# A global-filter layer and a two-layer network on one core: the inverse step of the next token group moves into a packed step of the third unit

## The chip, the cores and the metric

The kernel runs on one core of a Trainium2 chip. The metric is the device time in microseconds (us) of the program on that core. Engines are named as in the profile: PE is the matrix engine (PEld is its weight load), DVE the vector engine, ACT the scalar engine, POOL the GpSimd engine; SP issues most of the DMAs.

## The reference, cut to what matters

```python
X = np.fft.rfft(x, axis=1)                 # x: (8, 3008, 256)
Y = X * (filt_r + 1j * filt_i)[None]
t = np.fft.irfft(Y, n=3008, axis=1).reshape(24064, 256)
h = t @ w_in                               # (24064, 2048)
g = h - np.tanh(h)
out = g @ w_out                            # (24064, 256)
```

Everything is computed in float32.

## The kernel before

**The transform.** The length 3008 is split as 64 by 47, and the transform of a batch element is done in four stages with tables held in the kernel. The *forward* step (`first`, or in packed form `split_first`) transforms along the 64 and stores to the DRAM tensor `ct1`. The *middle* step (`middle`) takes a quarter of the frequencies at a time, o = 0 to 3: `packed` transforms along the 47 ("there"), the filter is multiplied in, and `packed` transforms back ("back") to the DRAM tensor `ct2`. The *inverse* step (`last`) transforms along the 64 back again and leaves the tokens of one group, transposed, in the tile `ut`; `combine` then makes four sums of its blocks, in `tu`.

**Packed steps.** `last`, `packed` and `split_first` use matmuls that fill only a part of the PE array: 64 by 64 (line 582, tile `pu`), 24 by 32 (line 401, tile `pm`) and 32 by 32 (line 340, tile `pm`), several of them side by side. All other matmuls of the main loop fill the array, 128 by 128. The program calls each Python matmul of float32 data as two instructions, so that a packed step of 32 matmuls shows as x64.

**Groups and units.** The main loop goes through 48 token groups, six chunks c for each of eight batch elements p. A group has 512 tokens (448 for c = 0) and its blocks are w = 256 (224) wide. A group is done in four units u = 0 to 3, each with a quarter of the hidden features, and U counts units. In unit U the loop interleaves, by hand, four streams:

- `up(U)`: the first matrix product, with seven block products in place of eight (a scheme of Strassen's kind). They run in the order 1, 2, 6, 5, 7, 4, 3 over the PSUM banks x, y, x, z, x, x, z. Bank x is added to step by step: after product 1 ACT copies it (`s1`), after 6 it copies it again (`u2`), after 7 once more (`u3`), and after 4 DVE does. All three ACT copies are line 629. The next product into bank x cannot begin until the copy before it has ended.
- `shrink(U-1)`: h - tanh(h) in the form h times a square: ACT runs an arctangent (line 735), a tanh (738) and a square (741) for each half of h, DVE multiplies (745), and POOL makes the four sums `t` (lines 603 to 606).
- `down(U-2)`: the second matrix product, again with seven products, into the banks o0 to o3 (line 795). Its four pieces, products (1, 2), (3, 5), (6, 7) and (4), are let in by the calls `d()`. In the last unit of a group the sums of these banks are taken off; line 834 is the last reader of bank o3.
- `t(k)`, k = 0 to 4: five places in a unit where a step of the transform for a later group or batch element is let in, and where four stores are issued on SP's queue.

What a place `t(k)` holds is fixed: the inverse step of the next group at (u, k) = (3, 2); "there" at (2, 0) and "back" at (1, 3), by the list `kinds`; the pieces of `split_first` at the places (c, u, k) of `SPLIT_AT`. In a unit the order at its start is: product 1, product 2, copy `s1`, `t(0)`, first `d()`, first activations (`shrinks`), and then product 6.

**Banks.** There are eight PSUM banks: x, y, z, t and o0 to o3. A packed step borrows four of them, the inverse step two.

**Weight sums.** The seven products need sums of weight blocks. `sums(u)` makes the four for one quarter of a weight matrix, on DVE (lines 228 and 231). Those of quarters 0, 1, 2 and 4 are made among the conversions of the weights, before unit 6; those of 3, 5, 6 and 7 in units 6 and 7.

Of the kernel before, what the change touches and what calls it, by code (L numbers as in the profile page):

```python
# [116 lines left out]
def kernel(  # L117
# [104 lines left out]

        return jobs

    def sums(u):

        w = (wu if u < 4 else wd)[:, :, 256 * (u % 4):256 * (u % 4) + 256]
        V.tensor_add(w[:, 4], w[:, 6], w[:, 3])
        yield
        for to, one_in, less in ((5, 4, 0), (2, 1, 5), (6, 0, 6)):  # L230
            V.tensor_sub(w[:, to], w[:, one_in], w[:, less])  # L231
            yield

    def begun(tiles, job, queue=nc.sync):
        j = converted(tiles, *job, queue)
# [5 lines left out]
    def weights(tiles, jobs, queue, began, ahead, after=()):  # L241

        began += [begun(tiles, job, queue) for job in jobs[len(began):ahead]]
        yield
        for k in range(len(jobs)):
            pending[0] = len(jobs) - k
            for n, _ in enumerate(began[k]):
                yield
                if (after or k > 1) and n == 2 and k + 1 < len(jobs):
                    next(began[k + 1])  # L250
            if k + ahead < len(jobs):
                began.append(begun(tiles, jobs[k + ahead], queue))
            pending[0] = len(jobs) - k - 1
            for u in dict(after).get(k, ()):
                yield from sums(u)

    def load_x(t, b, r, n):

# [47 lines left out]
    def split_first(b, z):  # L306

        quarters = [slice(32 * k, 32 * k + 32) for k in range(4)]
        for c, tags in enumerate((("t", "o1", "y", "o0"), ("t", "o3", "o1", "o2"),
                                  ("t", "o1", "y", "o0"))):  # L310
            f = tr.tile([128, XH, 128], F32, tag="f", bufs=2, name="f")[:, 0:2]
            f = f.rearrange("p a (b n) -> p (a b) n", n=32)
            nc.sync.dma_start(f, split_d[:, 256 * c:256 * c + 256])
            x0, x1 = (tr.tile([128, XH, DM], F32, tag="x", bufs=2, name="x_sb") for _ in range(2))
            for h, t in enumerate((x0, x1)):
                at = b * SEQ + 32 * h * NR
                for g in range(2):
                    r = 2 * FH * c + FH * g
                    low, high = quarters[g], quarters[2 + g]
                    nc.sync.dma_start(t[low], dram(x.tensor, (at + r) * DM,  # L320
                                                   [[NR * DM, 32], [1, FH * DM]]))
                    lo = int(r == 0)
                    if lo:
                        nc.sync.dma_start(t[high, 0], dram(x.tensor, at * DM,
                                                           [[NR * DM, 32], [1, DM]]))
                    nc.sync.dma_start(t[high, lo:FH], dram(x.tensor, (at + NR - r - lo) * DM,
                                                           [[NR * DM, 32], [-DM, FH - lo], [1, DM]]))
            yield
            both = tr.tile([128, 2, 2, DM], F32, tag="a1", bufs=1, name="a1")
            even = both.rearrange("p v n c -> p (v n) c")  # L330
            V.tensor_add(even, x0, x1)
            yield
            V.tensor_sub(x1, x0, x1)
            yield
            banks = z(tags)
            for n in range(2):
                for k, (bank, part) in enumerate(zip(banks, quarters)):
                    for j, to in enumerate(quarters):
                        m, odd = 2 * (j // 2) + n, j % 2
                        nc.tensor.matmul(bank[to, n], f[part, 2 * m + odd],  # L340
                                         (x1 if odd else even)[part, m], start=True, stop=True)
            made = both, x0.rearrange("p (v n) c -> p v n c", v=2)
            other = x1[:, 0:2]
            for g, a1 in enumerate(made):
                ACT.copy(a1[:, 1], banks[2 + g])
            ACT.copy(other, banks[1])
            for g, a1 in enumerate(made):
                V.tensor_add(a1[:, 0], other if g else banks[0], a1[:, 1])
                V.tensor_sub(a1[:, 1], other if g else banks[0], a1[:, 1])
                outs[:0] = [(dram(ct1[b], ((1 - j % 2) * NH + 2 * FH * c + FH * g +  # L350
                                           2 * (j // 2)) * DM,
                                  [[2 * NH * DM, 32], [64 * NH * DM, 2], [1, 2 * DM]]),
                             a1[part].rearrange("p v n c -> p v (n c)"))
                            for j, part in enumerate(quarters)]
                yield

    SPLIT_AT = {(0, 0, 2), (0, 1, 0), (0, 1, 3), (1, 1, 1), (1, 1, 4), (2, 0, 2),
                (3, 0, 2), (4, 2, 0), (4, 2, 2), (4, 3, 0), (5, 0, 2), (5, 1, 0), (5, 1, 3),
                (5, 2, 2)}

    def parts(t, b, g, first_block=0, n=4, step=1):
# [25 lines left out]
    def packed(banks, o, weight, data):  # L387

        ahead, whole, late = [], [], []
        for q, bank in enumerate(banks):  # L390
            part = slice(PAD * q, PAD * q + NH)
            for col in range(4):
                to, at = bank[PAD * col:PAD * col + PAD], data(q, col)[part]
                plain, special = (wide[part, weight(q, col, last)] for last in (0, 1))
                if o == 3 and 3 == (col if weight is WAYS[0] else q):
                    ahead.append((to[:, 0], plain, at[:, 0:DM]))
                    late.append((to[:, 1], special, at[:, DM:2 * DM]))
                else:
                    whole.append((to.rearrange("p n c -> p (n c)"), plain, at))
        for to, weights_of, at in ahead + whole + late:  # L400
            nc.tensor.matmul(to, weights_of, at, start=True, stop=True)  # L401
# [205 lines left out]

    hs, gs = {}, {}

    def up(U, d, e, s, t):  # L610

        i, u = divmod(U, 4)
        b, tu, w = uts[i]
        rhs = [b[0][0], b[1][0], b[1][1], tu[:, 3, 0:w], tu[:, 0, 0:w], tu[:, 1, 0:w],
               tu[:, 2, 0:w]]
# [24 lines left out]
        mm(X, 1, True)  # L640
        mm(Y, 2, True)
        s1 = copied("s1")
        t(0)
        d()
        shrinks(0)
        V.tensor_add(h[:, 0, :, 0:w], Y, s1)
        e()
# [358 lines left out]
    with tc.tile_pool(name="tr", bufs=2) as tr, tc.manual_schedule():  # L1006
# [16 lines left out]
        with tc.tile_pool(name="pro", bufs=1) as pro, \  # L1023
# [201 lines left out]
            for g in range(last_g + 1):  # L1225
# [30 lines left out]
                if g == 3:  # L1256
# [5 lines left out]
            next(fs)  # L1262
            convert(100)
            late = weights(tiles1, jobs[5:], G, ahead, 3,
                           after={6: (0,), 8: (1,), 10: (2, 4)})
            next(late)
            for _ in first1(x1):
                pass
# [2 lines left out]
        with tc.tile_pool(name="dn", bufs=2) as dn, \  # L1271
# [4 lines left out]

            def zd2(name, shape):
                return [ps.tile(shape, F32, tag=tag, bufs=1, name=name) for tag in "ty"]

            def zd4(tags):  # L1280
                return [ps.tile([128, 2, DM], F32, tag=tag, bufs=1, name="pm") for tag in tags]
# [59 lines left out]
            for U in range(total + 2):  # L1341
                i, u = divmod(U, 4)
                if U == 6:
                    assert not pending
                    late = (None for u in (3, 5, 6, 7) for _ in sums(u))
                if U == 3:
                    G.dma_start(mats[:, 0:10 * PAD], wide_d[0:KM])
                if U < total:
                    p, c = groups[i]
                    if c == 0 and u == 0 and 0 < p < BATCH - 1:  # L1350
                        plan += STAGES
                    if u == 0 and i + 1 < len(groups) and c + 1 < NC:
                        e2s[i + 1] = load_e2(*groups[i + 1])
                    if u == 2 and i + 1 < len(groups) and c + 1 == NC:
                        assert not plan
                        e2s[i + 1] = load_e2(*groups[i + 1])
                    if u == 3 and c + 1 == NC and p + 3 < BATCH:
                        firsts[p + 3] = split_first(p + 3, zd4)
                        next(firsts[p + 3])
                    if u == 3 and c + 1 == NC and p + 2 < BATCH:  # L1360
                        mids[p + 2] = middle(p + 2, zd4)
                        next(mids[p + 2])
# [11 lines left out]
                def d():  # L1374

                    next(dw, None)
# [10 lines left out]
                def t(k):  # L1387
# [7 lines left out]
                    if i == 1 and pos == LEAD - 7:  # L1395
# [1 line left out]
                        mids[1] = middle(1, zd4)  # L1397
                        next(mids[1])
                        plan.extend(STAGES)
                    if (u, k) == (3, 2) and i + 1 < len(groups):  # L1400
                        next(last(i + 1, z2))
                    elif due and due[0] <= pos and (U < 4 or u < 3 and k == 2):
                        due.pop(0)
                        next(firsts[2])
                    elif (c, u, k) in SPLIT_AT and 0 < p < BATCH - 2:
                        next(firsts[p + 2])
                    elif plan and plan[0] == kinds.get((u, k)):
                        plan.pop(0)
                        next(mids[p + 1])
# [58 lines left out]
```

## Time and profile before

| What | us |
|---|---|
| median of three runs | 2559.25 |
| lowest and highest run | 2557.61, 2559.39 |
| the profiled execution, its own time | 2556.2 |
| span of the profiled execution | 2554.4 |
| DVE busy | 1875.8 (73%) |
| ACT busy | 1667.1 (65%) |
| POOL busy | 1484.3 (58%) |

The busy time of PE and the other rows that the argument needs stand in the prediction. In the timelines each row has the start, the length, the engine, the line, the operation, what it writes and reads, and its shape with the number of merged instructions. A matmul's length is modelled and overlaps with the next one, so the distance between starts is what counts: four full matmul instructions of 256 columns start 0.86 us before the next four.

### The profile page before, as it was taken

The numbers are of one execution on the slowest core, as the hardware profiler recorded it, in microseconds if no ns is written. First come the engines' busy times: TensorE is split into PE (matmuls) and PEld (weight loads), VectorE is DVE, ScalarE is ACT, GpSimd is POOL, SyncE is SP. The second block draws the span as 40 slices with busy tenths as digits, with TensorE's granted clock in tenths as the row PEclk, the third lists the DMA queues.
The fourth block names the chain that finished last, engine by engine and source line by source line (L and its number), as shares of the span: only waits on it lengthen the run. The fifth ranks groups of instructions, "written<-read, shape, count | busy, mean of one in ns | idle before, by whom it ended". The sixth has DMA issues, their size and how long they took to land.

```text
span 2554.4 us, 44623 instructions
## 1 busy us (share of the span) xinstructions
PE 2535.7 (99%) x17072; PEld 2173.1 (85%) x17072; DVE 1875.8 (73%) x2262; ACT 1667.1 (65%) x2498; POOL 1484.3 (58%) x1129
## 2 busy tenths in 40 slices
PE   9999999999999999999999999999999999999998
PEld 8678889888898888988888888888889888898887
DVE  6887776887678876888668886688866777555555
ACT  4666666666666666666666666666666666666665
POOL 5356665666466665666555665566645666555552
PEclk9999999999999999999999999999999999999999
DMA  8963224322343323342233322443123322110110
GB/s 233 287 163 103 65 53 109 102 65 61 83 102 91 81 64 94 80 111 59 72 95 99 85 63 61 108 100 97 36 67 85 94 66 52 26 32 18 25 22 19
DMA packets 333828, 212.43 MB, mean 83 GB/s; under 512 B 231841, under 2 KB 304959, under 8 KB 329957
## 3 DMA queue, kind: packets, MB, share of 16 engines
q1 hardware_dynamic: 318471, 184.18, 29.3%
q0 software_dynamic: 11616, 17.44, 2.5%
q10 hardware_dynamic: 3518, 7.87, 0.9%
q8 instruction: 136, 2.23, 0.4%
q14 instruction: 87, 0.71, 0.1%
HBM read 128.75 MB, written 83.39 MB: 83 GB/s over the span
## 4 chain that ended last, share of the span: by engine, by line
PE 94%; DMA 3%; DVE 1%; ACT 1%; issue 0%; SPq 0%; POOL 0%; ACTq 0%; POOLq 0%; DVEq 0%
PE o L795 44%; PE x L623 25%; PE z L623 12%; PE y L623 6%; PE pm L401 3%; PE pu L582 2%; DMA x<-in_x_dram 1%; PE pm L340 1%; DMA filt<-in_filt_r_dram 1%; DMA ct<-a 0%; PE o L857 0%; PE pf L297 0%; DMA filt<-filt 0%; DMA ct<-e 0%; DVE wd L231 0%
## 5 line engine op out<-in xcount | busy, mean ns | idle before, releaser
L795 PE MATMUL o<-t,wd 128*128 128x256 f32 (+1 forms) x3008 | 763.4, 376 | 0.0
L603 POOL TENSOR_TENSOR t<-h 128x512 f32<-128x512 f32 (+1 forms) x186 | 305.4, 1642 | 712.7 <-DVE h L745 704.3
L745 DVE TENSOR_TENSOR h<-h,y 128x1024 f32<-128x1024 f32 (+1 forms) x384 | 580.2, 1511 | 160.1 <-ACT y L741 156.6
L795 PEld LDWEIGHTS o<-t,wd 128*128 128x128 f32 x3008 | 568.8, 190 | 85.8 <-POOL o L827 15.1
L623 PE MATMUL x<-tu,wu 128*128 128x256 f32 (+1 forms) x2256 | 576.1, 378 | 0.0
L795 PE MATMUL o<-h,wd 128*128 128x256 f32 (+1 forms) x2256 | 573.4, 377 | 0.2 <-DVE h L745 0.2
L795 PEld LDWEIGHTS o<-h,wd 128*128 128x128 f32 x2256 | 425.6, 190 | 71.3 <-issue 18.4
L629 ACT COPY s<-x 128x512 f32<-128x512 f32 (+1 forms) x188 | 108.6, 578 | 565.0 <-PE x L623 564.5
L623 PEld LDWEIGHTS x<-tu,wu 128*128 128x128 f32 x2256 | 423.3, 190 | 56.9 <-issue 3.9
L738 ACT ACTIVATE y<-y 128x1024 f32<-128x1024 f32 (+1 forms) x384 | 399.4, 1040 | 12.1
L741 ACT ACTIVATE y<-y 128x1024 f32<-128x1024 f32 (+1 forms) x384 | 399.9, 1041 | 4.6
L735 ACT ACTIVATE y<-h 128x1024 f32<-128x1024 f32 (+1 forms) x384 | 400.4, 1043 | 2.5 <-DVE h L671 1.7
L604 POOL TENSOR_TENSOR t<-h,t 128x512 f32<-128x512 f32 (+1 forms) x186 | 313.9, 1688 | 14.6
L606 POOL TENSOR_TENSOR t<-h,t 128x512 f32<-128x512 f32 (+1 forms) x186 | 303.8, 1633 | 0.0
L605 POOL TENSOR_TENSOR t<-h 128x512 f32<-128x512 f32 (+1 forms) x186 | 289.8, 1558 | 0.0
L629 ACT COPY u<-x 128x512 f32<-128x512 f32 (+1 forms) x376 | 213.3, 567 | 57.0 <-PE x L623 54.1
L671 DVE COPY h<-x 128x512 f32<-128x512 f32 (+1 forms) x188 | 127.8, 680 | 127.2 <-PE x L623 127.1
L623 PE MATMUL y<-ut,wu 128*128 128x256 f32 (+1 forms) x752 | 190.2, 375 | 0.7 <-ACT a L299 0.7
L623 PE MATMUL z<-tu,wu 128*128 128x256 f32 (+1 forms) x752 | 190.2, 375 | 0.4 <-DVE h L679 0.4
L623 PE MATMUL z<-ut,wu 128*128 128x256 f32 (+1 forms) x752 | 190.2, 375 | 0.4 <-DVE h L663 0.4
L623 PE MATMUL x<-ut,wu 128*128 128x256 f32 (+1 forms) x752 | 190.1, 375 | 0.0
L663 DVE TENSOR_TENSOR h<-z,u 128x512 f32<-128x512 f32 (+1 forms) x188 | 127.3, 677 | 72.0 <-ACT u L629 71.1
(208 smaller groups left out, 2809.1 us busy)
## 6 DMA issues: line engine op xcount, KB each, us to landing
ft<-filt SPq DMA_DIRECT2D x28, 1024.0 KB
ct<-nn SPq DMA_DIRECT2D x56, 512.0 KB
e<-ct SPq DMA_DIRECT2D x47, 512.0 KB
a<-ct SPq DMA_DIRECT2D x112, 192.0 KB
out_dram<-ot SPq DMA_DIRECT2D x1248, 16.0 KB
x_sb<-in_x_dram SPq DMA_DIRECT2D x110, 128.0 KB
ct<-a SPq DMA_DIRECT2D x60, 128.0 KB
ct<-x_sb SPq DMA_DIRECT2D x60, 128.0 KB
```

Source lines behind the costliest of these rows:

```text
L603: by.tensor_sub(t[0], b[0][1], b[0][0])
L604: by.tensor_sub(t[1], b[1][1], t[0])
L605: by.tensor_sub(t[2], b[1][1], b[0][1])
L606: by.tensor_sub(t[3], b[1][0], t[1])
L623: nc.tensor.matmul(bank[:, k], wu[:, q - 1, (2 * u + k) * 128:(2 * u + k + 1) * 128], rhs[q - 1], start=(first and k == 0), stop=True, ski ...
L629: ACT.copy(t, X)
L671: V.tensor_copy(h[:, 2, :, 0:w], X)
L735: ACT.activation(y[k], ht[k], AF.Arctan, scale=TURN)
L738: ACT.activation(y[k], y[k], AF.Tanh, scale=BEND)
L741: ACT.activation(y[k], y[k], AF.Square, scale=SCALE, accum_out=y_sums[:, 2 * U + k // 2:2 * U + k // 2 + 1])
L745: V.tensor_mul(ht[k], ht[k], y[k])
L795: nc.tensor.matmul(product(q), wd[:, q - 1, (2 * u + k) * 128: (2 * u + k + 1) * 128], rhs[q - 1][:, k], start=(u == 0 and k == 0 and q == ...
```

## The change

`merged(U)` is true for the third unit (u = 2) of the groups 2 to 46, but not of the group (0, 5). In such a unit `t(0)` and the first `d()` run ahead of products 1 and 2, and the inverse step of the next group is let in there, at (2, 0), in the banks y and x; the step that was at (2, 0) before follows it at once. In the other groups the inverse step stays at (3, 2), in the banks t and y. The packed order of "there" goes over the banks t, o1, o2, o3 and no longer over t, o3, o1, o2. The last piece of `split_first` with matmuls moves from (5, 1, 3) to (5, 2, 0), with other banks, and the first takes its banks in another order. The inverse step's operands `e2` are loaded at u = 0 of the group before, but for (0, 5). Of the weight sums, three of four for the quarters 3, 5, 6 and 7 are made among the conversions, and only the last of each, which overwrites a block that is in use until then, in unit 6.

```diff
-    def sums(u):
+    def sums(u, n=4):
...
-        for to, one_in, less in ((5, 4, 0), (2, 1, 5), (6, 0, 6)):
+        for to, one_in, less in ((5, 4, 0), (2, 1, 5), (6, 0, 6))[:n - 1]:
...
+    def last_sum(u):
+
+        w = (wu if u < 4 else wd)[:, :, 256 * (u % 4):256 * (u % 4) + 256]
+        V.tensor_sub(w[:, 6], w[:, 0], w[:, 6])
...
-        for c, tags in enumerate((("t", "o1", "y", "o0"), ("t", "o3", "o1", "o2"),
-                                  ("t", "o1", "y", "o0"))):
+        for c, tags in enumerate((("t", "y", "o1", "o0"), ("t", "o3", "o1", "o2"),
+                                  ("t", "o3", "o1", "o2"))):
...
-                (3, 0, 2), (4, 2, 0), (4, 2, 2), (4, 3, 0), (5, 0, 2), (5, 1, 0), (5, 1, 3),
+                (3, 0, 2), (4, 2, 0), (4, 2, 2), (4, 3, 0), (5, 0, 2), (5, 1, 0), (5, 2, 0),
...
-        for q, bank in enumerate(banks):
+        for q in (0, 2, 3, 1) if weight is WAYS[0] else range(4):
+            bank = banks[q]
...
+    def merged(U):
+
+        i, u = divmod(U, 4)
+        return u == 2 and 1 < i < len(groups) - 1 and groups[i] != (0, NC - 1)
...
         i, u = divmod(U, 4)
+        if merged(U):
+            t(0)
+            d()
...
         s1 = copied("s1")
-        t(0)
-        d()
+        if not merged(U):
+            t(0)
+            d()
...
-                           after={6: (0,), 8: (1,), 10: (2, 4)})
+                           after={6: ((0, 4),), 8: ((1, 4),),
+                                  10: ((2, 4), (4, 4), (3, 3), (5, 3), (6, 3), (7, 3))})
...
+            def z2u(name, shape):
+                return [ps.tile(shape, F32, tag=tag, bufs=1, name=name) for tag in "yx"]
...
-                    late = (None for u in (3, 5, 6, 7) for _ in sums(u))
+                    late = (last_sum(u) for u in (3, 5, 6, 7))
...
-                    if u == 0 and i + 1 < len(groups) and c + 1 < NC:
-                        e2s[i + 1] = load_e2(*groups[i + 1])
-                    if u == 2 and i + 1 < len(groups) and c + 1 == NC:
-                        assert not plan
+                    at = (2, 0) if merged(4 * i + 2) else (3, 2)
+                    if i + 1 < len(groups) and u == (2 if (p, c) == (0, NC - 1) else 0):
+                        assert c + 1 < NC or not plan
                         e2s[i + 1] = load_e2(*groups[i + 1])
...
-                    if (u, k) == (3, 2) and i + 1 < len(groups):
-                        next(last(i + 1, z2))
+                    behind = i + 1 < len(groups) and (u, k) == at
+                    if behind:
+                        next(last(i + 1, z2 if u == 3 else z2u))
+                    if behind and u == 3:
+                        pass
                     elif due and due[0] <= pos and (U < 4 or u < 3 and k == 2):
```

More of the change, by code (lines that the diff above doesn't have):

```diff
@@ L253, in weights @@
             pending[0] = len(jobs) - k - 1
-            for u in dict(after).get(k, ()):
-                yield from sums(u)
+            for u, n in dict(after).get(k, ()):
+                yield from sums(u, n)
     def load_x(t, b, r, n):
```

## The prediction, made before the changed kernel ran

> **What bounds the kernel now.** I read the page first, then the chain of waits, then the list of waits, then the timelines of PE, ACT and DVE in one third and fourth unit.
>
> ```profile
> span 2554.4 us, 44623 instructions
> PE 2535.7 (99%) x17072; PEld 2173.1 (85%) x17072; DVE 1875.8 (73%) x2262; ACT 1667.1 (65%) x2498; POOL 1484.3 (58%) x1129
> PE 94%; DMA 3%; DVE 1%; ACT 1%; issue 0%; SPq 0%; POOL 0%; ACTq 0%; POOLq 0%; DVEq 0%
> ```
>
> PE is busy nearly all of the span and carries 94% of the chain, so what counts is PE's own sequence: how much a packed step costs beyond its data, and where PE waits. A part of PE's busy time is such overhead, since the ends of matmuls are modelled; starts show it. The timeline of PE in the third unit (from 1394.94) and the fourth (from 1408.37) of a steady group:
>
> ```profile
> 1391.19 1.03 PE L623 MATMUL x<-tu,wu 128*128 128x256 f32 x4
> ...
> 1393.21 1.02 PE L795 MATMUL o<-t,wd 128*128 128x224 f32 x4
> 1394.08 1.03 PE L623 MATMUL z<-ut,wu 128*128 128x256 f32 x4
> 1394.94 1.03 PE L623 MATMUL x<-ut,wu 128*128 128x256 f32 x4
> 1395.80 1.03 PE L623 MATMUL y<-ut,wu 128*128 128x256 f32 x4
> 1396.76 1.22 PE L401 MATMUL pm<-a,mats_sb 24*32 24x512 f32 x32
> 1397.91 1.99 PE L795 MATMUL o<-h,wd 128*128 128x256 f32 x8
> 1399.74 1.03 PE L623 MATMUL x<-tu,wu 128*128 128x256 f32 x4
> ...
> 1408.37 1.03 PE L623 MATMUL x<-ut,wu 128*128 128x256 f32 x4
> 1409.23 1.03 PE L623 MATMUL y<-ut,wu 128*128 128x256 f32 x4
> ...
> 1414.85 0.59 PE L795 MATMUL o<-t,wd 128*128 128x256 f32 x2
> 1415.37 1.16 PE L582 MATMUL pu<-gt,e 64*64 64x64 f32 x64
> 1416.46 1.13 PE L623 MATMUL x<-tu,wu 128*128 128x256 f32 x4
> 1417.43 1.89 PE L795 MATMUL o<-t,wd 128*128 128x256 f32 x8
> ```
>
> From 1408.37 to 1409.23 four full instructions take 0.864, 0.216 each. Taking these off, the inverse step costs 1417.43 - 1414.85 - 6 x 0.216 = 1.28 "there" 1399.74 - 1395.80 - 12 x 0.216 = 1.35, and the "back" step in the gap of the first rows (four instructions of 224 columns take 0.756) 1394.08 - 1391.19 - 0.864 - 0.756 = 1.27. The data alone, at 0.216 for 256 columns, would take 64 x 0.054 / 4 = 0.86 for the first (four 64 by 64 parts side by side) and 32 x 0.432 / 16 = 0.86 for the second. So a packed step carries 0.41 to 0.49, about 0.21 for each seam, going in and coming out.
>
> **The pairs.** 44 units are merged. In 37 the inverse step meets a packed step: groups 2 to 4 (3), six in each of p = 1 to 5 (30), four in p = 6. In the other 7 (p = 6, c = 4 and 5; p = 7, c = 0 to 4) it stands alone and has two seams as before. No row shows a 64 by 64 step beside a 24 by 32 or 32 by 32 one. Apart, a pair has four seams. If the inner seam costs nothing, two go: 0.42 saved. If the inner one costs as much as both that it replaces, nothing is saved. I take the value of the nearest rows, one full seam inside: three left, 0.21 saved. The Trainium skill, TensorEngine Tiling (Array Packing), Key Properties, says that a change of the tiling mode drains the array; 64 by 64 to 32 by 32 is such a change, and by that rule the inner seam stays and a pair saves 0.21, while without it the pair would save 0.42. No run here shows it yet.
>
> In the five pairs with c = 0 of p = 1 to 5 I count no gain, because bank o3 comes late there:
>
> ```profile
> 1347.67 0.92 PE L623 MATMUL y<-ut,wu 128*128 128x224 f32 x4
> 1348.52 1.47 PE L401 MATMUL pm<-a,mats_sb 24*32 24x512 f32 x32
> 1349.92 1.78 PE L795 MATMUL o<-h,wd 128*128 128x224 f32 x8
> 1351.54 0.92 PE L623 MATMUL x<-tu,wu 128*128 128x224 f32 x4
> ```
>
> ```profile
> 1348.30 0.42 DVE L834 TENSOR_TENSOR o<-o,p 128x256 f32<-128x256 f32 x1
> ...
> 1395.70 0.39 DVE L834 TENSOR_TENSOR o<-o,p 128x224 f32<-128x224 f32 x1
> ```
>
> At 224 columns (0.189 each, 0.756 for four) "there" costs 1351.54 - 1347.67 - 12 x 0.189 = 1.60 here, since the last reader of o3 ended at 1348.72, after the step began. That reader is queued on DVE behind work of the second unit, which the change doesn't touch, so o3 still comes at 1348.72. The merged "there" could start after half a seam, the inverse step and the inner seam, 0.1 + 0.86 + 0.21 = 1.17 behind the place of product 1 (1347.67 - 0.756 = 1346.91), at 1348.1; it finishes about when it did, even with o3 last in its order. In the other groups o3 is free at 1396.09, and the merged "there" comes at 1394.94 + 1.17 = 1396.1: just in time, o3 being last. Pairs: 32 x 0.21 = 6.7 less, between 0 and 13.4. The new bank order may also take off the 0.08 by which "there" (1.35) exceeds "back" (1.27); for the 12 such steps (c = 1 and 2 of p = 1 to 6) I take half, 0.5, between 0 and 1.
>
> **The chain on ACT.** The other side of the change is the place of the first `d()`. Before, 8 instructions of `down` lay between product 2 and product 6. In a merged unit they come before product 1, so from product 1 to product 7 PE has only products 1, 2, 6, 5 and one `d()`: 4 x 0.864 + 1.728 = 5.18. Product 7 waits for ACT's second copy, which lies behind the first copy and three activations. The timeline of ACT in the same fourth unit:
>
> ```profile
> 1409.44 0.58 ACT L629 COPY s<-x 128x512 f32<-128x512 f32 x1 [3.03 <-PE x L623]
> 1409.92 1.06 ACT L735 ACTIVATE y<-h 128x1024 f32<-128x1024 f32 x1
> 1411.01 1.06 ACT L738 ACTIVATE y<-y 128x1024 f32<-128x1024 f32 x1
> 1412.10 1.06 ACT L741 ACTIVATE y<-y 128x1024 f32<-128x1024 f32 x1
> ...
> 1413.15 0.57 ACT L629 COPY u<-x 128x512 f32<-128x512 f32 x1
> ```
>
> ACT was idle until product 1 was done, then ran without a gap; the copy ended at 1413.72, 5.35 after product 1 began at 1408.37. In a merged unit ACT has the copies of both packed steps in front (two or three of 0.58 beside the one of the inverse step), but three are done within 1.8 us of the pair's end, while the first `d()` and product 1 take 1.73 + 0.86 = 2.6; so ACT is idle again when product 1 ends and 5.35 holds. That is later than 5.18. What a late copy costs, these rows of another third unit show, where three copies of `split_first` had held ACT up:
>
> ```profile
> 944.27 0.59 PE L795 MATMUL o<-t,wd 128*128 128x256 f32 x2
> 944.82 1.13 PE L623 MATMUL x<-tu,wu 128*128 128x256 f32 x4
> 945.79 1.46 PE L795 MATMUL o<-t,wd 128*128 128x256 f32 x6
> ```
>
> ```profile
> 944.21 0.56 ACT L629 COPY u<-x 128x512 f32<-128x512 f32 x1
> ...
> 946.72 0.56 ACT L629 COPY u<-x 128x512 f32<-128x512 f32 x1
> ```
>
> The copy ended at 944.77, 0.07 after product 7 could have begun (944.27 + 2 x 0.216 = 944.70). Product 7 began 0.12 late, and the next row 945.79 - 944.82 - 0.864 = 0.10 later still: 0.22 for a lateness of 0.07, so lateness plus 0.15. A merged unit of 256 pays 5.35 + 0.15 - 5.18 = 0.32. Product 6 now comes 1.73 after product 1, and the first copy ends at 1.65: that costs 0.07 which the wait of product 7 contains. For 224 columns:
>
> ```profile
> 1359.11 0.92 PE L623 MATMUL x<-ut,wu 128*128 128x224 f32 x4
> ```
>
> ```profile
> 1363.41 0.51 ACT L629 COPY u<-x 128x448 f32<-128x448 f32 x1
> ```
>
> 1363.92 - 1359.11 = 4.81 against 6 x 0.756 = 4.54: 0.42. Sum: 37 x 0.32 + 7 x 0.42 = 14.8 more. The five units like that at 944.82 had paid 0.22 already: 13.7 more. Nothing later makes up for it, as PE is the bound. The third copy does not add: it comes 2.51 after the second (946.72 + 0.56 against 944.77), while products 7 and (6, 7) take 2.59.
>
> **The weight sums.** The list of waits has three in unit 7 that lie behind sums on DVE:
>
> ```profile
> PE pu L582 <- DVE h L646: 0.8, 1, 0.8
> PE z L623 <- DVE h L679: 0.4, 1, 0.4
> PE z L623 <- DVE h L663: 0.4, 1, 0.4
> ```
>
> ```profile
> 165.32 0.42 DVE L231 TENSOR_TENSOR wu<-wu 128x256 f32<-128x256 f32 x1
> ...
> 176.50 1.39 DVE L231 TENSOR_TENSOR wd<-wd 128x256 f32<-128x256 f32 x1
> ```
>
> Each costs its idle time plus 0.27 (0.17 of modelled end, 1.03 against 0.864, and 0.10 for the next row): 2.4 to 2.5 in all. The change takes 12 of these 16 sums into unit 5, where at 0.42 each (the quick ones; one beside other work took 1.39) they are 5 us of DVE; two of them come ahead of the DVE copy of bank x, which may cost 0.2. I count 2.3 less, between 1 and 2.5.
>
> **Moves that I cost at nothing.** The `e2` load keeps its place at u = 0 in most groups, with two units (13.4 us each, 1394.94 to 1408.37) until its use and no longer more than three; for c = 5 it comes earlier. On SP's queue only stores lie around it. The two DVE operations on `ut` and POOL's four sums for `tu` move forward by some two thirds of a unit; POOL is busy for 58% and has its next work, the sums `t`, only at the unit's end. DVE is busy for 73%, and the operations lie in front of all DVE work of the third unit; what hides them are its gaps, and if these are gone, the read of bank z comes late and product 3 waits, which is a rival below. Bank y must be read before product 2; the second packed step, `d()` and product 1 lie between, 0.86 + 1.73 + 0.86 = 3.4 for one ACT copy and two DVE operations.
>
> **The sum.** -6.7 - 0.5 + 13.7 - 2.3 = +4.2 on the profiled execution's 2556.2, whose span is 2554.4. The three timed runs have a median 3.05 above that execution; I add the 4.2 to the median: 2563.5.
>
> **The rivals.**
> - *No inner seam.* The parts of the two steps run into each other, 0.42 saved a pair: -13.4 - 0.5 + 13.7 - 2.3 = -2.5, 2556.8. For it: all tiles are small and need little weight to be loaded. Against: every seam in the trace costs.
> - *The merge saves nothing*, the inner seam costing two: +10.9, 2570. For it: 64 by 64 is a shape of its own, with its own way in and out.
> - *It gains* because the ACT chain is hidden after all and the other terms stand: -6.7 - 0.5 - 2.3 - 1.1 = -10.6, 2548.7. It would take an ACT chain under 5.03 us from product 1. Against: the chain had no gap in it and its lengths are fixed.
> - *Slower by a new wait on DVE.* The third unit's DVE work delays the read of bank z, and product 3 waits. Product 3 comes 0.15 + 0.864 + 1.728 + 0.864 + 0.864 = 4.5 after the end of ACT's second copy, the read can begin 2.5 after it, so it decides once DVE comes to the read more than about a microsecond late. At the smallest price seen, 0.22, in each of 44 units: +9.7, in all +13.9, 2573. For it: DVE's 73% is a mean, and the third unit now has more. Against: the list of waits names DVE only in unit 7.
>
> **How the numbers follow.** Forecast 0.52 (2563.5, own range 2560 to 2567), no inner seam 0.15, nothing saved 0.15, hidden chain 0.07, DVE 0.11. What a measurement can tell from no change is 0.2%, 5.1 us. The forecast lies just inside; two fifths of it (0.21) count as slower. Slower: 0.21 + 0.15 + 0.11 = 0.47. Faster: 0.07 and 0.02 of the seamless case. The same: 0.44. The range, 2555 to 2571, takes in both ends of the seam and leaves out the hidden chain and most of the DVE case.
>
> **What would show it.** In the changed profile a merged pair should cost about 2.4 in place of 2.55 to 2.65; 2.2 means no inner seam. Product 7 of a merged unit should start 0.05 after the end of ACT's second copy and 5.4 after product 1, and the list of waits or the chain should show ACT there. The three waits of unit 7 should be gone. I am wrong if product 7 comes 5.18 after product 1, if "there" waits inside the pair for o3 in groups other than c = 0, or if product 3 waits for DVE.

## The result and the profile after

| | before | after |
|---|---|---|
| median, us (14 runs each) | 2558.97 | 2563.28 |
| lowest and highest run, us | 2555.81, 2566.16 | 2561.24, 2570.57 |
| the profiled execution, its own time, us | 2556.2 | 2563.13 |

The ratio of after to before is 1.002, with an interval of 1.0013 to 1.0027, that is 3.3 to 6.9 us. The change makes the kernel slightly slower, by 4.3 us in the medians. From the page of the changed kernel:

```profile
span 2561.4 us, 44532 instructions
PE 2540.3 (99%) x17072; PEld 2165.8 (85%) x17072; DVE 1865.0 (73%) x2262; ACT 1665.7 (65%) x2498; POOL 1465.9 (57%) x1129
PE 94%; DMA 3%; DVE 1%; ACT 1%; issue 0%; POOL 0%; ACTq 0%; SPq 0%; POOLq 0%; DVEq 0%
```

PE does the same 17072 instructions, and the shares hardly move: as before, only the starts on PE tell something. In the changed kernel `up`'s matmuls are line 637, `down`'s 810, the inverse step 588, "there" and "back" 407, ACT's copies of bank x 643. The timeline of PE for the third unit of the same group as in the prediction (start, length, engine, line, what is written and read, shape, count):

```profile
1397.01 1.03 PE L637 MATMUL z<-ut,wu 128*128 128x256 f32 x4
1397.97 1.16 PE L588 MATMUL pu<-gt,e 64*64 64x64 f32 x64
1399.06 1.16 PE L407 MATMUL pm<-a,mats_sb 24*32 24x512 f32 x32
1400.14 1.99 PE L810 MATMUL o<-h,wd 128*128 128x256 f32 x8
1401.98 1.03 PE L637 MATMUL x<-ut,wu 128*128 128x256 f32 x4
1402.84 1.03 PE L637 MATMUL y<-ut,wu 128*128 128x256 f32 x4
1403.70 1.11 PE L637 MATMUL x<-tu,wu 128*128 128x256 f32 x4
1404.65 1.03 PE L637 MATMUL z<-tu,wu 128*128 128x256 f32 x4
...
1407.38 1.13 PE L637 MATMUL x<-tu,wu 128*128 128x256 f32 x4
1408.34 1.89 PE L810 MATMUL o<-t,wd 128*128 128x256 f32 x8
```

The pair: 1401.98 - 1397.01 - 12 x 0.216 = 2.38, where the two steps apart cost 1.28 + 1.35. Product 7 starts 1407.38 - 1401.98 = 5.40 after product 1, and the next row 1408.34 - 1407.38 - 0.864 = 0.10 late. ACT in the same unit, and the list of PE's waits (its weight load stands in front of the matmul):

```profile
1403.04 0.59 ACT L643 COPY s<-x 128x512 f32<-128x512 f32 x1 [1.69 <-PE x L637]
...
1406.76 0.56 ACT L643 COPY u<-x 128x512 f32<-128x512 f32 x1
```

```profile
PEld x L637 <- ACT u L643: 17.1, 46, 0.4
...
PEld x L637 <- ACT s L643: 9.4, 44, 0.2
```

ACT's second copy ends at 1407.32, 5.34 after product 1, and product 7 follows 0.06 later. The wait for the first copy comes 44 times, once for each merged unit; before, the list had for the two copies together only this:

```profile
PEld x L623 <- ACT u L629: 2.4, 8, 0.4
```

From product 1 of unit 9 to that of unit 190 the trace has 2303.99 us before and 2311.50 after, 7.5 more; the weight sums lie ahead of this stretch. Taken apart by starts on PE, with 0.216 and 0.189 for each full instruction, 13.8 more lie at products 6 and 7 of the third units, and 6.3 less at the packed steps and their seams.

### The profile page after: what moved, and what is told of

Same layout as the page of the kernel before. It is cut to its first block, busy times and chain, and to the rows that moved or that the text cites. A ratio compares the mean times of both kernels' runs of the same rounds, so it can differ in the third digit from the quotient of the medians.

```text
span 2561.4 us, 44532 instructions
## 1 busy us (share of the span) xinstructions
PE 2540.3 (99%) x17072; PEld 2165.8 (85%) x17072; DVE 1865.0 (73%) x2262; ACT 1665.7 (65%) x2498; POOL 1465.9 (57%) x1129
## 4 chain that ended last, share of the span: by engine, by line
PE 94%; DMA 3%; DVE 1%; ACT 1%; issue 0%; POOL 0%; ACTq 0%; SPq 0%; POOLq 0%; DVEq 0%
PE o L810 44%; PE x L637 25%; PE z L637 12%; PE y L637 6%; PE pm L407 3%; PE pu L588 2%; DMA ct<-a 1%; PE pm L345 1%; DMA x<-in_x_dram 1%; DMA filt<-in_filt_i_dram 0%; DMA filt<-in_filt_r_dram 0%; DMA filt<-filt 0%; PE pf L302 0%; PE o L872 0%; DVE nn L439 0%
## 5 line engine op out<-in xcount | busy, mean ns | idle before, releaser
L609 POOL TENSOR_TENSOR t<-h 128x512 f32<-128x512 f32 (+1 forms) x186 | 304.3, 1636 | 844.3 <-DVE h L760 833.6
L760 DVE TENSOR_TENSOR h<-h,y 128x1024 f32<-128x1024 f32 (+1 forms) x384 | 573.5, 1494 | 222.8 <-ACT y L756 222.7
L810 PEld LDWEIGHTS o<-t,wd 128*128 128x128 f32 x3008 | 568.8, 190 | 84.5 <-POOL o L842 15.1
L610 POOL TENSOR_TENSOR t<-h,t 128x512 f32<-128x512 f32 (+1 forms) x186 | 314.9, 1693 | 14.6
L612 POOL TENSOR_TENSOR t<-h,t 128x512 f32<-128x512 f32 (+1 forms) x186 | 314.6, 1691 | 0.0
L611 POOL TENSOR_TENSOR t<-h 128x512 f32<-128x512 f32 (+1 forms) x186 | 264.7, 1423 | 0.0
```

What stands on the lines that cost most here:

```text
L609: by.tensor_sub(t[0], b[0][1], b[0][0])
L610: by.tensor_sub(t[1], b[1][1], t[0])
L611: by.tensor_sub(t[2], b[1][1], b[0][1])
L612: by.tensor_sub(t[3], b[1][0], t[1])
L760: V.tensor_mul(ht[k], ht[k], y[k])
L810: nc.tensor.matmul(product(q), wd[:, q - 1, (2 * u + k) * 128: (2 * u + k + 1) * 128], rhs[q - 1][:, k], start=(u == 0 and k == 0 and q == ...
```

## The experiments

**The first `d()` back behind product 1.**

```diff
         if merged(U):
             t(0)
-            d()
...
         mm(X, 1, True)
+        if merged(U):
+            d()
         mm(Y, 2, True)
```

> The changed kernel with one thing undone: in a merged unit only the two packed steps stand ahead of product 1; the first d() is again behind product 1, ahead of product 2, so that 8 matmul instructions more lie between products 1 and 7. Theory (the ACT chain): product 1 to product 7 becomes 4 x 0.864 + 2 x 1.728 = 6.91 us in place of 5.40, ACT's second copy (5.35 after product 1) is long done, the rows that name ACT before product 7 go from the list of waits, and 37 x 0.32 + 7 x 0.42 = 14.8 us go: 2563.3 - 14.8 = about 2548.5, ratio to the kernel before 0.996. Product 1 has then nothing of PE between it and the packed steps, so a late read of banks x and y could take some of that back; they are used by the inverse step first, some 1.2 us before its end. Rival 1 (what the merged unit loses is lost in the packed steps or in bank order, and the wait for ACT only shows it): the time stays at 2560 or more. Rival 2 (product 1 or 2 now waits for the reads of banks x and y): ACT's row goes, but a row of about 0.3 us a unit appears before product 1 or 2, and the time is 2555 to 2563.

Measured: 2554.66, ratio to before 0.998 (0.9971 to 0.999). The rows that name ACT before product 7 are gone. Products 1 and 7 in the unit shown above:

```profile
1393.46 1.13 PE L636 MATMUL x<-ut,wu 128*128 128x256 f32 x4
...
1400.47 0.81 PE L636 MATMUL x<-tu,wu 128*128 128x256 f32 x3
```

They are 7.01 apart, the 6.91 of the expectation and 0.10 of the seam behind the packed step. From unit 9 to 190 the trace has 15.1 us less at products 6 and 7 than in the changed kernel, so the chain on ACT is what the place of `d()` costs. But the kernel gains only 8.6. The list of waits and the timelines of PE and ACT in one of the last merged units show what took the rest:

```profile
PE x L636 <- ACT odd L592: 4.9, 7, 0.7
```

```profile
2208.05 1.03 PE L636 MATMUL z<-ut,wu 128*128 128x256 f32 x4
2209.01 1.16 PE L588 MATMUL pu<-gt,e 64*64 64x64 f32 x64
2210.88 1.13 PE L636 MATMUL x<-ut,wu 128*128 128x256 f32 x4 [0.70 <-ACT odd L592]
```

```profile
2210.24 0.59 ACT L592 COPY odd<-pu 128x512 f32<-128x512 f32 x1 [3.68 <-PE pu L588]
```

Seven times the inverse step stands alone, and product 1 comes right behind it into bank x, which ACT reads until 2210.83. Such a step costs 2.06 in place of 1.29: 7 x 0.775 = 5.4 lost. Rival 2 was right for these 7 units, and wrong for the 37 in which the other packed step covers the read.

**Product 1 between the two packed steps.**

```diff
-        if merged(U):
-            t(0)
...
-        mm(X, 1, True)
         if merged(U):
+            t(0, lambda: mm(X, 1, True))
             d()
+        else:
+            mm(X, 1, True)
```

(This stands on the kernel with the first `d()` back; `t` runs what it is given between the inverse and the other packed step.)

> The same as the kernel with the first d() back behind product 1, but in a merged unit product 1 runs between the inverse step and the other packed step, so that the two are not neighbours: inverse step, product 1, packed step, first d(), product 2. Everything else is equal, so the difference of the two kernels is the worth of the packed step joining. Theory (one seam of about 0.2 us is saved by a direct neighbour): 32 to 37 pairs x 0.19 to 0.21 = 6.1 to 7.8 us slower than the joined one, about 2555. Rival with no inner seam (two seams saved): 32 x 0.42 = 13.4 slower, about 2562. Rival where joining saves nothing: 0 to 1 us slower, about 2549. In the trace an inverse step between full matmuls costs 1.28 and the other 1.27 to 1.35 beyond the full instructions, against 2.375 for the joined pair.

Measured: 2586.76, 32 above the joined one, more than any of the three allowed. The list of waits has the reason:

```profile
PE x L634 <- ACT odd L592: 31.0, 44, 0.7
```

Now product 1 waits for bank x in all 44 units, 0.7 each. So the time alone can't price the seam; it shows that the inverse step's bank must be covered by other work before product 1, and that the packed step behind it does that. The starts on PE do price the seam. The third unit shown above, with the two steps apart:

```profile
1407.38 1.03 PE L634 MATMUL z<-ut,wu 128*128 128x256 f32 x4
1408.33 1.16 PE L588 MATMUL pu<-gt,e 64*64 64x64 f32 x64
1410.20 1.13 PE L634 MATMUL x<-ut,wu 128*128 128x256 f32 x4 [0.70 <-ACT odd L592]
1411.26 1.14 PE L407 MATMUL pm<-a,mats_sb 24*32 24x512 f32 x32
1412.33 1.99 PE L811 MATMUL o<-h,wd 128*128 128x256 f32 x8
1414.16 1.03 PE L634 MATMUL y<-ut,wu 128*128 128x256 f32 x4
```

From product 3 of the unit before to product 2 it is 1414.16 - 1407.38 = 6.78 here, and 1396.15 - 1390.33 = 5.82 in the kernel with the steps joined. The difference is 0.96 or 0.97 in each of the 32 pairs outside c = 0. The same wait costs 0.775 where the inverse step stands alone (2.06 in place of 1.29), so 0.19 is left for the joining: one seam. In the five pairs with c = 0 only 0.33 separates the two kernels, since joined these cost 3.0.

**No merged unit.**

```diff
-        return u == 2 and 1 < i < len(groups) - 1 and groups[i] != (0, NC - 1)
+        return False
```

> The changed kernel without any merged unit: the inverse step stays at (3, 2) in all groups; the bank order of the packed steps, the moved piece of the split step and the sooner weight sums are kept. Theory: only the small terms are left, the sums (0.9 by the trace of the changed kernel, 2.3 by the prediction's price) and the bank order (0 to 1): 1 to 3 us under the kernel before, 2556 to 2558, ratio 0.999 to 1.000. Rival (the loss lies in the bank order, the moved split piece or the sooner sums): 2562 or more. If a unit c = 0 gains from o3 being last in its order, the five such steps, at 1.60 before, should come to 1.3 to 1.4 and give up to 1.5 us more.

Measured: 2556.92, ratio 0.9987 (0.9977 to 0.9998), as the theory had it: the small terms together give 2.0 in the medians. The trace doesn't bear all of this out: the spans are 2554.4 before and 2554.1 here, and from unit 9 to 190 this kernel takes 2305.09, 1.1 more than the one before. The moved piece of `split_first` costs that: its copies make product 7 wait for ACT in five third units (c = 5) that had no such wait before, 0.22 each. The five "there" steps of c = 0 come to 1.50, from 1.60, and not to the 1.3 to 1.4 that o3's last place might have given; those of c = 1 and 2 (p = 1 to 6) gain nothing from the new bank order (1.36 to 1.40, from 1.34 to 1.35).

**The old weight sums.**

```diff
-                                  10: ((2, 4), (4, 4), (3, 3), (5, 3), (6, 3), (7, 3))})
+                                  10: ((2, 4), (4, 4))})
...
-                    late = (last_sum(u) for u in (3, 5, 6, 7))
+                    late = (None for u in (3, 5, 6, 7) for _ in sums(u))
```

> The changed kernel with the weight sums as they were before: all 16 of the quarters 3, 5, 6 and 7 in the units 6 and 7. By the trace of the changed kernel: three waits of unit 7 return (0.8, 0.4 and 0.4 us of idle time, 2.5 us in all), and the wait of 1.4 us before a product into bank x in unit 5 (for the DVE copy of that bank, 1.6 us in all) goes: 0.9 slower than the changed kernel. By the prediction's price: 2.3 slower. The two differ by less than the runs can tell; the waits in the profile decide, and the place of PE in unit 10: 0.9 or 2.3 us later than in the changed kernel.

Measured: 2564.6, 1.3 over the changed kernel. The three waits are back:

```profile
PE pu L588 <- DVE h L661: 0.8, 1, 0.8
...
PE z L637 <- DVE h L694: 0.4, 1, 0.4
PE z L637 <- DVE h L678: 0.4, 1, 0.4
```

In the changed kernel they are replaced by one wait in unit 5, which this run doesn't have. PE and DVE of the changed kernel there:

```profile
144.12 1.03 PE L637 MATMUL z<-ut,wu 128*128 128x256 f32 x4
146.52 1.13 PE L637 MATMUL x<-ut,wu 128*128 128x256 f32 x4 [1.37 <-DVE h L686]
```

```profile
144.98 0.42 DVE L228 TENSOR_TENSOR wu<-wu 128x256 f32<-128x256 f32 x1
145.44 0.42 DVE L231 TENSOR_TENSOR wu<-wu 128x256 f32<-128x256 f32 x1
145.78 0.68 DVE L686 COPY h<-x 128x512 f32<-128x512 f32 x1
```

Two of the sooner sums stand ahead of the DVE copy of bank x, and product 1 waits for that copy until 146.46. From product 1 of unit 4 to that of unit 9 the trace has 73.55 with the old sums and 72.16 with the new: 1.4 gained, not 2.3; it falls between the two sizes that had been set against each other. These are single executions. The kernel before, with the old sums too, takes 73.46 for this stretch, and five other kernels with the new sums take 71.63 to 73.37, so the gain can be anything from 0.1 to 1.9; the medians' 1.3 is not clear of noise either.

**The order without the merge.**

```diff
-                    at = (2, 0) if merged(4 * i + 2) else (3, 2)
+                    at = (3, 2)
```

> The changed kernel with its order in the third unit (the packed step and the first d() ahead of product 1), but with the inverse step left at (3, 2) in all groups. Against the changed kernel only the place of the inverse step differs, so the difference is the worth of the two packed steps being neighbours; against the kernel without merged units only the order differs, so that difference is the price of the chain on ACT alone. Theory (ACT chain): product 7 waits for ACT's second copy in 44 units though nothing is merged, 0.32 each (0.42 in those of 224 columns), 13.7 to 14.8 over the 2556.9 of the kernel without merged units: 2570.6 to 2571.7. By the same theory, with one seam of 0.18 to 0.20 saved in 32 pairs and 0.2 lost in 5, the changed kernel is 5 to 7 under it. Rival 1 (the ACT wait comes from the second packed step in front, whose copies hold ACT up): no wait, 2557 to 2560. Rival 2 (joining saves nothing): 2563 to 2564, as the changed kernel; rival 3 (joining saves two seams): 2575 or more.

Measured: 2610.1, ratio 1.0196 (1.018 to 1.0212), 39 above what the theory had. Both rows of the list of waits matter:

```profile
PEld pm L407 <- DVE o L849: 22.9, 27, 1.0
PEld x L637 <- ACT u L643: 17.1, 46, 0.4
```

The second row is that of the changed kernel, and product 7 is again 5.40 behind product 1 (4.87 for 224 columns) in 42 of the 44 units, though one packed step at most stands in front. So rival 1 falls: the wait for ACT comes from the order alone, and over the kernel without merged units it is worth 12.9 (from unit 9 to 190). In the other two, units 74 and 122, product 7 comes 0.63 and 0.16 later still: in this trace the granted clock was 0.5 for 3.4 us in each of two stretches, from 1060.6 and from 1692.0, and next to their like the units there lose 3.4 in all. Of the remaining 39, that takes 3.4; 3.6 lie at the first `d()` of the seven units without a packed step, which now waits for DVE's multiplication (line 760); and 32 lie at the packed steps. PE and DVE in the same third unit as above:

```profile
1422.94 1.03 PE L637 MATMUL z<-ut,wu 128*128 128x256 f32 x4
1423.89 2.17 PE L407 MATMUL pm<-a,mats_sb 24*32 24x512 f32 x32
```

```profile
1424.56 0.38 DVE L849 TENSOR_TENSOR o<-o,p 128x224 f32<-128x224 f32 x1
```

"There" begins as soon as the unit does, and bank o3 has its last reader until 1424.94: the step takes 2.17 in place of 1.16. The first row of the list counts 27 such waits before "there"; `split_first` has the other 10. So this run can't price the seam. It shows what none of the theories had named: in a merged unit the inverse step is the cover for the last reader of o3, which products 1 and 2 were before.

**Merged units only where there is a pair** (with the first `d()` back behind product 1).

```diff
-        return u == 2 and 1 < i < len(groups) - 1 and groups[i] != (0, NC - 1)
+        return u == 2 and 1 < i < 40 and groups[i] != (0, NC - 1)
```

> The changed kernel with the first d() back behind product 1, and merged units only where a packed step is there to be joined: in the 7 groups from (6, 4) on, where the inverse step stood alone at (2, 0), it is back at (3, 2). With the first d() back, product 1 came right behind these lone inverse steps and waited for ACT to read bank x, 2.06 us for a step in place of 1.29. Theory: 7 x 0.775 = 5.4 go, 2554.7 - 5.4 = 2549.2, ratio to the kernel before 0.996. Rival (the shortfall of that kernel, 8.6 gained in place of 14.8, lies elsewhere, in the 37 real pairs): 2553 or more.

Measured: 2549.7, ratio 0.9959 (0.9945 to 0.9973). The wait for `odd` is gone from the idle time of the matmuls, and the forecast of 2549.2 holds. This kernel against that without merged units is the trial of the merge by itself, since here no unit pays for ACT: from unit 9 to 190 it takes 2296.37 against 2305.09, 8.7 less. 2.2 of that are late copies at product 7 which the other kernel has in 10 units; 6.5 are the packed steps and their seams. Against the kernel before, 2303.99, it is 7.6 less.

**The sums let in later, and the DVE work of c = 0 out of the way.** The first edit stands on the kernel before it, the second on both.

```diff
             for u, n in dict(after).get(k, ()):
+                if (u, n) == (3, 3):
+                    for _ in range(PAUSE):
+                        yield
                 yield from sums(u, n)
```

```diff
             ACT.copy(other, banks[1])
+            if c == 0:
+                yield
             for g, a1 in enumerate(made):
...
-    SPLIT_AT = {(0, 0, 2), (0, 1, 0), (0, 1, 3), (1, 1, 1), (1, 1, 4), (2, 0, 2),
+    SPLIT_AT = {(0, 0, 2), (0, 1, 0), (0, 1, 3), (0, 1, 4), (1, 1, 1), (1, 1, 4), (2, 0, 2),
```

(`PAUSE` is 4.)

> The kernel with merged units only at real pairs, and the sooner weight sums let in four steps later, so that the DVE copy of bank x in unit 5 comes ahead of them. Theory: the wait of 1.4 us for that copy goes, 1.6 in all, 2547.6. Rival (the sums then fall on another wait, in unit 6 or 7): no gain, 2549.

> The kernel with the later weight sums, and for c = 0 the DVE operations of split_first, which stood in the third unit's way to the last reader of bank o3, moved to a place of their own at (0, 1, 4), behind that reader. Theory: the five pairs of c = 0, 3.01 now, come to the 2.38 that the pair (6, 0) costs, 5 x 0.63 = 3.1 less, about 2544.5. Rival (that reader is late for another reason): the five pairs stay at 2.8 to 3.0 and the time at 2547.

Measured: 2547.55, ratio 0.9954 (0.9941 to 0.9968), and 2545.3, ratio 0.9942 (0.9929 to 0.9956). With the later sums the wait in unit 5 is gone from the list; in the kernel that this edit stands on it was 0.9, not the 1.4 of the changed kernel. The time is the forecast one, but the step of 2.2 in the medians, where 1.6 was forecast, is not clear of noise: the two intervals overlap, and from unit 4 to unit 9 the trace gains 72.27 - 71.49 = 0.8. For c = 0, first PE in the changed kernel, then DVE there:

```profile
1348.54 0.92 PE L637 MATMUL z<-ut,wu 128*128 128x224 f32 x4
1349.39 1.16 PE L588 MATMUL pu<-gt,e 64*64 64x64 f32 x64
1350.48 1.79 PE L407 MATMUL pm<-a,mats_sb 24*32 24x512 f32 x32
1352.20 1.78 PE L810 MATMUL o<-h,wd 128*128 128x224 f32 x8
1353.82 0.92 PE L637 MATMUL x<-ut,wu 128*128 128x224 f32 x4
```

```profile
1348.34 0.69 DVE L353 TENSOR_TENSOR a<-pm,a 128x512 f32<-128x512 f32 x1 [1.42 <-ACT a L350]
1349.13 0.69 DVE L354 TENSOR_TENSOR a<-pm,a 128x512 f32<-128x512 f32 x1
1349.74 1.08 DVE L760 TENSOR_TENSOR h<-h,y 128x896 f32<-128x896 f32 x1
1350.74 0.42 DVE L849 TENSOR_TENSOR o<-o,p 128x256 f32<-128x256 f32 x1
```

and the same place in the last kernel, where lines 353 and 849 are 359 and 856:

```profile
1341.00 1.16 PE L594 MATMUL pu<-gt,e 64*64 64x64 f32 x64
1342.15 1.15 PE L413 MATMUL pm<-a,mats_sb 24*32 24x512 f32 x32
```

```profile
1340.35 0.42 DVE L856 TENSOR_TENSOR o<-o,p 128x256 f32<-128x256 f32 x1 [0.83 <-PE o L817]
1340.69 0.68 DVE L359 TENSOR_TENSOR a<-pm,a 128x512 f32<-128x512 f32 x1
```

Two operations of `split_first` had waited for ACT at the head of DVE's queue, and the last reader of o3 behind them ended at 1351.16, after "there" had begun. Moved behind it, the reader ends before the unit's first packed step, and "there" takes 1.15, not 1.79. Such a pair falls from 3.01 to 2.44, 2.9 us for all five, and from unit 9 to 190 the trace falls by as much, 2296.36 - 2293.50; the medians moved by 2.25, and their intervals overlap. The last kernel is 13.4 us under the kernel before the change (2558.65 beside it) and is the fastest of all here.

## Why the prediction was right

The time, +4.2 predicted and +4.3 measured, came from a sum whose largest term was right to 0.1 and whose smaller terms were off by 1.8 together.

- *The chain on ACT*, 13.7: 13.8 in the trace. Product 7 came 5.40 behind product 1 and 0.06 behind ACT's copy, as written. That it is the place of `d()` and no property of the merged steps is shown by two runs: with `d()` back it goes, with the merge undone and the order kept it stays. The rival with a hidden chain is refuted.
- *The pairs*, 6.7 and 0.5 for the bank order: 6.3 in the trace, in two parts. A joined "there" costs 2.38 against 1.29 + 1.27 for the two undisturbed steps alone, so one inner seam stays and 0.18 is saved (0.20 for `split_first`, 2.71 against 1.29 + 1.62). The kernel with the steps apart gives the same 0.19. This refutes both the rival without a seam, which wanted 2.2, and the one that saves nothing. With the bank order the 32 pairs gave 6.9; the order alone gave nothing at c = 1 and 2; the 0.08 by which "there" had exceeded "back" goes only with the inverse step in front. The prediction weighed the rule of the Trainium skill, TensorEngine Tiling (Array Packing), Key Properties, that a change of the tiling mode drains the array. The trace agrees with it: one seam stays where the mode changes inside the pair. That the change of mode is what costs is not shown, as no run joins two steps of the same mode.
- *The pairs with c = 0*, counted as nothing: 0.12 lost in each, 0.6 in all. The step that failed is that the merged "there" "finishes about when it did". It did so within 0.1, but before, products 1 and 2 were done by then, 8 x 0.189 = 1.51, while now only the inverse step is, which saves 1.29 elsewhere. Ending at the same time is a loss of 0.22, less what o3's last place gained. The last experiment shows that the late reader of o3 is its whole cause but for 0.06.
- *The weight sums*, 2.3: 1.3 by the medians and 1.4 by the trace, inside the bounds of 1 and 2.5, though neither is firm, as the experiment says. The mis-sized term is the two sums ahead of the DVE copy of bank x, priced at 0.2; they caused a wait of 1.37.
- *Just in time for o3* in the other groups: right. In the changed kernel the weight load of "there" waits for line 849 five times, as many as there are pairs with c = 0. How much hangs on it was not seen: without the inverse step in front, the packed steps cost 32 us more.
- *A late read of bank z*: product 3 starts on time in all merged units, so this rival is refuted.

By the trace the terms make 13.8 - 6.3 - 1.4 = 6.1, at the upper end of what the runs show (3.3 to 6.9); the profiled executions differ by 6.9, the medians by 4.3. That the forecast hit the median to 0.2 is therefore partly luck.

## What to carry to other kernels

When work is moved ahead of a product, count what is left between that product and the next one that needs its bank: here 5.18 us of matmuls against 5.35 of ACT work turned a saving of some 8 by the trace (6.3 at the packed steps, 1.4 at the sums) into a loss of 6, or 4.3 in the medians. With that one call put back, and three other waits cleared, the same merge gave a kernel 0.6% faster than before. Work in front of a unit is also a cover: each run that moved or removed a packed step without looking for the bank that it hid (bank x behind a lone inverse step, o3 behind product 2) paid 0.7 to 0.9 us a unit in the mean. A step that ends "at the same time" in a new order is no saving until what else had been done by then is counted.

## What was not expected of the hardware

A wait on PE costs more than its idle time, and it costs something before the releaser is late. In the third unit shown first, ACT's first copy ends at 1403.63, 0.08 before product 6 could begin (1401.98 + 1.73 = 1403.71), and product 6 begins on time at 1403.70; yet the next product comes 1404.65 - 1403.70 - 0.864 = 0.09 late. At product 7, by then due at 1404.65 + 0.864 + 1.728 = 1407.24, the copy ends at 1407.32: 0.08 late, the product starts 0.14 late, and the row behind it loses 0.10 more. The list of waits counts both, 44 times 0.2 and 44 times some 0.4, as idle time of the weight load, and the matmuls themselves show no idle time at all in these units.
